# First block's gate and value products in unsplit float32, and a front in a new order

## The chip, the cores and the metric

One core of a Trainium2 chip runs the kernel. The metric is the device time of one execution in microseconds; lower is better.

## The reference

A chunked state-space scan makes an array of 3072 tokens by 256 features, and a gated unit follows. All of it is float32.

```python
def _attn_ref(x, a, B, C):            # x (4,8,768,32), a (4,8,768), B and C (4,8,768,16)
    log_a = np.log(np.clip(a, 1e-06, 1.0))
    for c in range(nc):               # chunks of 32 steps
        cum = np.cumsum(la, axis=-1)
        L = np.exp(cum[:, :, :, None] - cum[:, :, None, :]) * causal
        M = np.einsum('bhin,bhjn->bhij', Cc, Bc) * L
        y_intra = np.einsum('bhij,bhjd->bhid', M, xc)
        y_inter = np.einsum('bhin,bhnd->bhid', Cc, state) * np.exp(cum)[..., None]
        y[:, :, sl] = y_intra + y_inter
        state = decay_full * state + np.sum(Bx, axis=2)   # Bx: B times x, decayed to the chunk's end
def _moe_ref(x, w_gate, w_val, w_out):                    # 256 -> 1536 -> 256
    g = x @ w_gate
    silu = g * (1.0 / (1.0 + np.exp(-g)))
    return (silu * (x @ w_val) @ w_out)
```

## The kernel before

**Blocks.** The 768 steps are cut into NB = 6 blocks of 128 steps; a block holds the 4 batches, so T = 512 tokens. Inside a block the scan works on K = 2 pieces of Q = 64 steps. For each block there are three stages: the attention, the gate and value products with SiLU and their product (NF = 12 units of 128 hidden features), and the output product (12 units, two halves of the output features).

**The attention of a block.** The decays a come as rows. For blocks 0 and 1 they are loaded small (`load_rows`), clipped, spread over the partitions by a float32 matmul against a 0/1 matrix `pick` (`spread`, the records "a") and scanned from PSUM by VectorE in halves (`scan_spread`) into L (decay between two steps) and E (decay from the piece's start). For blocks 2 to 5 the clipped rows are written to DRAM once (`load_all`, `clip_all`, `write_all`) and then loaded broadcast over the partitions (`load_aj`, `load_an`) and scanned there (`scan_j`, `scan_n`). `scores` makes S from B and C, C split by heads into Cz (`heads_apart`); `mix` multiplies S into L; `sums` makes the pieces' own states st from B weighed by the decay (`weigh_b`); `apart` and `step` make the running states T; `values` and `carried` add up y in PSUM, the latter with C weighed by E (`weigh_c`). All matmuls of the attention are float32 on small tiles.

**The split products.** The gated unit works in fp32r, a shorter float. Each operand is split into a high and a low part, and a product is three matmuls: high by high, low by high, high by low. For x that is `x_high` and `x_low`. The weights come as packed 8-byte numbers, in 18 pieces of 512 KB: 12 gate/value pieces (wg0 to wg11) and 6 output pieces (wo0 to wo5). Each goes through `w_magnitude`, `w_range`, `w_rest`, `w_shift`, `w_sign`, `w_round` to a float32 tile "w", then `w_high` and `w_low`; four or five of these must be VectorE's, the others may be ScalarE's. The hidden activations sg are split as well (`hid_high`, `hid_low`) just ahead of the output product.

**Order.** A planner (`Plan`) writes the order of the instructions by a list schedule: each operation has an engine or a choice of two, a cost, a rank (about the time when it is due), what it needs, and which buffers of a pool it takes and gives back. The engines then run their instructions in that fixed order, each waiting on semaphores. `due` and `due_sum` give the ranks of the products: blocks 0 and 1 form a group, and their gate products alternate unit by unit, so that a weight piece is used twice when it is ready; then come both output stages, and after these the blocks one at a time. `idle` puts filler matmuls on a tile of ones ("rest") into TensorE's stream, in groups of 6; `IDLE = 7, 12` groups. All loads go through SyncE's queue. All calls pass through one wrapper, so every row of the trace has its line, 192, and groups are told apart by their tiles: gv are the gate and value sums, po the output sums.

Of the kernel before, what the change touches and what calls it, by code (L numbers as in the profile page):

```python
# [29 lines left out]
SG = 21  # L30
# [172 lines left out]
def scan_moe_kernel(ctx: ExitStack, tc, aj, an, bc, xb, wgv, wo, cst, sel, out):  # L203
# [23 lines left out]
    pick = const.tile([K * BATCH, BATCH + 1, P], F32, name="pick")  # L227
# [4 lines left out]
    bl = [dict() for _ in range(NB)]  # L232
# [8 lines left out]
    def load_rows(k):  # L241

        t = moe.tile([K * BATCH, 2, T + 32], F32, tag="xl", name=f"rows{k}")
        t = bl[k]["rows"] = t[:, :, : H * W]
        sp.dma_start(t[:, 0], aj[k].rearrange("q (b c) -> (q b) c", b=BATCH))
        sp.dma_start(t[:, 1], an[k])
# [47 lines left out]

    def scan(t, d):

        ve.tensor_tensor_scan(t, t, d, 0.0, ALU.mult, ALU.add)

    def clip_rows(k, i):
        clip(bl[k]["rows"][:, i].rearrange("p (g t) -> p g t", t=W)[:, :, 1:])  # L300
# [3 lines left out]
    def spread(k, b, i):  # L304

        t = bl[k]["spread", b, i] = ps_at.tile([P, HALF], F32, tag="at", name=f"a{k}_{b}_{i}")
        src = bl[k]["rows"][:, b // BATCH, HALF * i : HALF * i + HALF]
        te.matmul(t, pick[:, b], src, start=True, stop=True)

    def scan_spread(k, b, i):  # L310
        if b < BATCH:
            to, d = bl[k]["L"][:, H * b : H * b + H], dj
        else:
            to, d = bl[k]["E"].rearrange("p b q t -> p (b q) t"), dn
        to, d = (t.rearrange("p g t -> p (g t)") for t in (to, d))
        half = slice(HALF * i, HALF * i + HALF)
        ve.tensor_tensor_scan(to[:, half], bl[k]["spread", b, i], d[:, half], 0.0, ALU.mult, ALU.add)
# [26 lines left out]
    def weigh_c(k):  # L344
        t = bl[k]["C"].rearrange("p b (q i) -> p (b q) i", i=Q)
        E = bl[k]["E"].rearrange("p b q t -> p (b q) t")
        ve.tensor_tensor(out=t, in0=t, in1=E[:, :, :Q], op=ALU.mult)

# [74 lines left out]
    def values(k, b):  # L423

        c = bl[k]
        if not b:
            c["y"] = [
                t[:, : BATCH * Q].rearrange("p (b i) -> p b i", i=Q) for t in banks(k, "y", 2 * K)
            ]
        L = c["L"].rearrange("p (b h) t -> p b h t", h=H)  # L430
        for g in range(2):
            for h in range(4 * g, 4 * g + 4):
                for q in range(K):
                    o = D * (h % 4)
                    te.matmul(
                        c["y"][2 * q + g][o : o + D, b], c["x"][piece(q), b, D * h : D * h + D],
# [19 lines left out]
    def new_x(k):  # L456
        xh[k] = moe.tile([P, 2, T], F32R, tag="xh", name=f"xh{k}")
        t = moe.tile([P, 2, T + 32], F32R, tag="xl", name=f"xl{k}")
        xl[k] = t.rearrange("p g t -> p (g t)")[:, : 2 * T].rearrange("p (g t) -> p g t", g=2)

# [27 lines left out]
    def w_magnitude(i, e):  # L488
        w = part[i]["w"] = raw.tile([P, 4 * P], I32, tag="w", name=f"{pieces[i][4]}w")
# [101 lines left out]
    def idle(n, i):  # L591
# [3 lines left out]
        for _ in range(6):  # L595
# [3 lines left out]
    load_rows(0)  # L599
    sp.dma_start(pick, sel)  # L600
    sp.dma_start(cs, cst)
    warm = const.tile([P, 1], F32, name="warm")
# [6 lines left out]
    def do(f, *a):  # L609
# [4 lines left out]
        dict(mm=4, at=4, L=1, E=1, bc=1, xb=1, Cz=1, T=2, tmp=2, raw=3, w=3, x=2, hh=HB, sg=SG, ob=2),  # L614
        dict(SP=3.0, Act=3.0, DVE=1.0, PE=1.5, Pool=2.0, **{"-": 0.0}),
# [6 lines left out]
    begin, t = {}, FIRST  # L622
    for g in groups:
        for i, k in enumerate(g):
            begin[k] = (t, i, len(g))
        t += len(g) * NF * ((GV if g[0] else PACE0) + PO) + len(g) * ATT

    def due(k, f=0):

        t, i, n = begin[k]  # L630
        return t + (f * n + i) * (GV if k > 1 else PACE0)

    def due_sum(k, f):
        t, i, n = begin[k]
        return t + n * NF * (GV if k > 1 else PACE0) + (i * NF + f) * PO

    add("-", 0.0, lambda: None, -9, gives="pick", lag=0.2)
    add("Act", 0.6, lambda: se.copy(dj, eye.unsqueeze(1).to_broadcast([P, H, W])), -9, ["cs"], gives="dj")
    add("-", 0.0, lambda: None, -9, gives="cs", lag=0.4)


    for n, many in enumerate(IDLE):
        for i in range(many):
            need = [("idle", n, i - 1)] if i else [("M", 0, 0)] if n else []
            takes = [] if i else [("at", ("rest", n))]
            add("PE", 0.37, do(idle, n, i), i if not n else 15 + i, need, takes=takes, uses=[("rest", n)], gives=("idle", n, i), kind="r")


    for i in range(NW):
        r = due(0, i) - 1.0 if i < NF else due_sum(0, 2 * (i - NF)) - 1.0  # L650
        add("SP", 0.48, do(w_fetch, i), r - 9.0, takes=[("raw", ("raw", i))], gives=("raw", i), lag=1.75)
        add([("Act", 0.6), ("DVE", 0.335)], None, do(w_magnitude, i), r - 5.5, [("raw", i)], takes=[("w", ("w", i))], gives=("mag", i))
# [4 lines left out]
        add("DVE", 0.6, do(w_round, i), r - 3.3, [("sign", i), ("rest", i)], uses=[("raw", i)], gives=("round", i))  # L657
        add([("Act", 0.6), ("DVE", 0.36)], None, do(w_high, i), r - 2.7, [("round", i)], gives=("wh", i))
# [165 lines left out]
```

## Time and profile before

| | us |
|---|---|
| runs, median of 3 (lowest, highest) | 375.75 (374.13, 378.84) |
| profiled execution | 375.97 |
| its span, first to last instruction | 374.2 |
| busy in the span: TensorE, weight loads, VectorE, ScalarE | 364.0, 288.9, 231.3, 129.3 |

The span is what the trace covers; 1.77 us of the profiled execution lie outside it. Busy shares are means over stages that have different limits, and a busy TensorE may still be running at its lower clock level, so equal instructions of different stretches have to be compared by their lengths.

### The profile page before, as it was taken

To read this page: it belongs to the slowest core of one execution; us is meant where nothing else is said; L and a number is where in the kernel's file an instruction comes from. 1 tells how busy PE (TensorE), PEld (TensorE's weight loads), DVE (VectorE), ACT (ScalarE), POOL (GpSimd) and SP (SyncE) were. 2 spreads that over 40 slices of the span, in tenths; PEclk is the share of its full clock that TensorE was granted. 3 is DMA by queue.
4 is the path that set the end of the run, shared out by engine and by line. 5 is a ranking of instruction groups with operands and counts; after the bars stand their busy time and mean duration, and the time that the engine had idled before them with its cause. 6 is when DMAs were issued, how large, how long until landed. Compare 5 with 4: busy or idle time off the path is not lost.

```text
span 374.2 us, 7684 instructions
## 1 busy us (share of the span) xinstructions
PE 364.0 (97%) x3342; PEld 288.9 (77%) x3342; DVE 231.3 (62%) x416; ACT 129.3 (35%) x230; POOL 0.8 (0%) x6
## 2 busy tenths in 40 slices
PE   7999998899999999899999999999999999999996
PEld 5677676687878877687778887788887788888896
DVE  4789996899997545269548564447763445262241
ACT  3244354366633542223134222134212134222142
POOL 0000000000000000000000000000000000000000
PEclk9999999999999999699999999999999999999999
DMA  6233169634400100560055100064100000100001
GB/s 258 90 103 154 60 182 232 175 116 145 134 0 0 58 0 34 156 154 2 4 164 121 57 0 2 4 176 108 56 3 2 2 2 0 56 2 0 0 2 56
DMA packets 8193, 26.81 MB, mean 72 GB/s; under 512 B 952, under 2 KB 1848, under 8 KB 7648
## 3 DMA queue, kind: packets, MB, share of 16 engines
q1 hardware_dynamic: 8160, 26.33, 23.5%
q8 instruction: 26, 0.43, 0.5%
q14 instruction: 7, 0.06, 0.1%
HBM read 22.98 MB, written 3.35 MB: 70 GB/s over the span
## 4 chain that ended last, share of the span: by engine, by line
PE 78%; DVE 14%; DMA 4%; issue 2%; ACT 0%; SPq 0%; DVEq 0%; ACTq 0%
PE gv L192 38%; PE po L192 27%; PE y L192 4%; DMA wg8r<-in_wgv 4%; PE a L192 4%; DVE sg L192 2%; PE rest L192 2%; PE S L192 2%; DVE L L192 2%; PE st L192 1%; DVE wo4w L192 1%; DVE wg5w L192 1%; DVE wo5w L192 1%; DVE wg11w L192 1%; DVE wg8w L192 1%
## 5 line engine op out<-in xcount | busy, mean ns | idle before, releaser
L192 DVE TENSOR_TENSOR sg<-gv,sg 128x512 f32<-128x512 f32 x72 | 49.8, 692 | 77.2 <-PE gv L192 77.1
L192 ACT ACTIVATE sg<-gv 128x512 f32<-128x512 f32 x72 | 42.5, 594 | 94.0 <-PE gv L192 93.9
L192 DVE TENSOR_TENSOR hl<-sg,hh 128x512 fp32r<-128x512 f32 x72 | 49.4, 689 | 29.0 <-ACT hh L192 28.5
L192 ACT CAST hh<-sg 128x512 fp32r<-128x512 f32 x58 | 36.1, 623 | 56.7 <-PE po L192 27.9
L192 DVE TENSOR_TENSOR_SCAN L<-L,dj 128x520 f32<-128x520 f32 x16 | 19.7, 1239 | 5.0 <-DMA L<-clipped 5.0
L192 PE MATMUL a<-rows,pick 8*128 8x260 f32 x40 | 16.1, 539 | 0.9 <-DVE rows L192 0.9
L192 DVE TENSOR_TENSOR L<-S,L 128x512 f32<-128x512 f32 x24 | 15.1, 685 | 2.8 <-PE S L192 2.8
L192 ACT COPY ob<-po 128x512 f32<-128x512 f32 (+1 forms) x13 | 7.2, 555 | 21.3 <-PE po L192 20.8
L192 DVE TENSOR_TENSOR_SCAN L<-a,dj 128x260 f32<-128x260 f32 x16 | 10.9, 694 | 4.3 <-PE a L192 4.2
L192 PE MATMUL y<-L,xb 64*32 64x64 f32 x768 | 11.9, 236 | 1.8 <-issue 1.3
L192 PE MATMUL rest<-unit 128*128 128x128 bf16 x114 | 11.8, 273 | 1.1 <-DVE warm L192 1.1
L192 PEld LDWEIGHTS <-unit 128*128 128x128 bf16 x114 | 9.2, 124 | 4.5 <-issue 3.3
L192 PEld LDWEIGHTS a<-rows,pick 8*128 8x128 f32 x40 | 9.1, 252 | 4.4 <-DVE rows L192 1.2
L192 PEld LDWEIGHTS y<-L,xb 64*32 64x32 f32 x768 | 7.9, 112 | 4.3 <-issue 1.7
L192 PEld LDWEIGHTS y<-bc,T 32*64 32x64 f32 x352 | 7.5, 140 | 4.3 <-issue 2.6
L192 PE MATMUL y<-bc,T 32*64 32x64 f32 x352 | 10.5, 239 | 0.0
L192 PE MATMUL po<-hh,wo0h 128*128 128x512 f32 (+1 forms) x26 | 9.8, 377 | 0.2 <-DVE sg L192 0.2
L192 PE MATMUL po<-hh,wo4h 128*128 128x512 f32 (+1 forms) x26 | 9.9, 382 | 0.0
L192 PE MATMUL po<-hh,wo3h 128*128 128x512 f32 (+1 forms) x26 | 9.9, 382 | 0.0
L192 PE MATMUL po<-hh,wo5h 128*128 128x512 f32 (+1 forms) x26 | 9.8, 378 | 0.0
L192 ACT ACTIVATE Cz<-bc,cs 128x512 f32<-128x512 f32 x10 | 6.7, 716 | 8.8 <-DMA bc<-in_bc 8.8
L192 PE MATMUL po<-hl,wo4h 128*128 128x512 f32 (+1 forms) x26 | 9.7, 374 | 0.0
(258 smaller groups left out, 823.0 us busy)
## 6 DMA issues: line engine op xcount, KB each, us to landing
xb<-in_xb SPq DMA_DIRECT2D x6, 768.0 KB, 7.5
L<-clipped SPq DMA_DIRECT2D x8, 520.0 KB, 7.8
bc<-in_bc SPq DMA_DIRECT2D x6, 512.0 KB, 3.7
out<-ob SPq DMA_DIRECT2D x11, 256.0 KB, 2.0
E<-clipped SPq DMA_DIRECT2D x4, 260.0 KB
wg0r<-in_wgv SPq DMA_DIRECT2D x1, 512.0 KB, 6.1
wg1r<-in_wgv SPq DMA_DIRECT2D x1, 512.0 KB
wg2r<-in_wgv SPq DMA_DIRECT2D x1, 512.0 KB
```

What stands on the lines that cost most here:

```text
L192: ins = getattr(self.engine, name)(*a, **k)
```

## The change

Block 0 runs its gate and value products alone and first. They take x as plain float32 copies of y (`x_whole`) and the rounded weights "w" as they are, in two float32 matmuls in place of six fp32r ones. The high and low parts of the gate weights are made later, before block 1's products, and `w_low` then waits for block 0's product with that piece. Until then the piece's float32 tile sits in the pool of the hidden activations (sg, 22 buffers in place of 21). The order of the large stages becomes: gate 0, gate 1, output 0, output 1, gate 2, output 2, and so on.

In the front, only batches 0 to 2 of block 0's L are spread by matmuls; batch 3 and E are loaded broadcast from the input and clipped and scanned in place. Block 1 uses the loads from DRAM like the later blocks. Block 0's bc and xb are issued from ScalarE's queue. The copy of `dj` goes from ScalarE to VectorE. `values` of block 0 runs in two halves by heads, each after two of the four `mix`. `weigh_c` of block 0 covers only the second piece. The filler groups have 3 matmuls in place of 6, in another number and at other ranks (46 groups in all). Block 2's attention and its loads get earlier ranks, the loads behind the fetch of piece 14.

```diff
-SG = 21
+SG = 22
...
+    def load_first_aj():
+        t, c = bl[0]["L"][:, H * SPREAD :], SPREAD * H * W
+        for q in range(K):
+            sp.dma_start(
+                t[piece(q)].rearrange("p g t -> p (g t)"),
+                aj[0, q, c:].unsqueeze(0).to_broadcast([Q, BATCH * H * W - c]),
+            )
+    def load_first_an():
+        sp.dma_start(
+            bl[0]["E"].rearrange("p b q t -> p (b q t)"),
+            an[0].unsqueeze(1).to_broadcast([H, N, BATCH * K * W]),
+        )
...
-        sp.dma_start(t, bc[k])
+        (sp if k else se).dma_start(t, bc[k])
...
-        sp.dma_start(t, xb[k])
+        (sp if k else se).dma_start(t, xb[k])
...
+    def x_whole(i, e):
+        copy(e, x_part(whole[0], i), bl[0]["y"][i])
...
     def gate_val(k, f, m):
+        if not k:
+            w = part[f]["w"].bitcast(F32).rearrange("p (a b c) -> p a b c", b=2, c=P)
+            for kc in range(2):
+                te.matmul(t, w[:, m, kc], whole[0][:, kc], start=not kc, stop=kc == 1)
+            return
         runs = [(w, x, kc) for w, x in ((wgh, xh), (wgl, xh), (wgh, xl)) for kc in range(2)]
...
-        for _ in range(6):
+        for _ in range(3):
             te.matmul(rest[n], unit, unit, start=True, stop=True)
...
-    GV, PO, ATT = 2.82, 1.41, 5.0
-    FIRST, PACE0 = 16.0, 3.2
-    groups = [(0, 1), *((k,) for k in range(2, NB))]
+    GV, PO, ATT, FIRST, PACE0 = 2.82, 1.41, 5.0, 17.0, 3.75
+    for k in range(NB):
+        begin[k] = t
+        t += (NF * GV if k else NF * PACE0) + ATT
+        for i in (() if not k else (0, 1) if k == 1 else (k,)):
+            begin_sum[i] = t
+            t += NF * PO
...
+        if i < NF:
+            r = due(1, i) - LATER
         add([("Act", 0.6), ("DVE", 0.36)], None, do(w_high, i), r - 2.7, [("round", i)], gives=("wh", i))
-        add("DVE", 0.6, do(w_low, i), r - 1.5, [("wh", i)], uses=[("w", i)], gives=("wl", i))
+        whole_done = [("gv", 0, i, m) for m in range(2)] if i < NF else []
+        add("DVE", 0.6, do(w_low, i), r - 1.5, [("wh", i), *whole_done], uses=[("w", i)], gives=("wl", i))
...
-        if k < 2:
-            z = (-5, 17)[k]
+        z = -5 if not k else r + LEAD[min(k, 3)]
...
-            z = r - 44 + 22 * (k == 2)
...
+        late = [("raw", LATE[k])] if k in LATE else []
...
-IDLE = 7, 12
+SPREAD = 3
+IDLE = [-9.0] * 8 + [-3.1, -3.0, -2.9, -2.8] + [0.5 * i for i in range(10)], [15.0 + 0.5 * i for i in range(24)]
+ALL, LATER = 16.0, 3.0
+LEAD = {1: -30.0, 2: -44.0, 3: -44.0}
+LATE = {2: NF + 2}
```

## Rows read from the trace of the kernel before

**Rows 1.** Stretches: window, length, busy us of PE, PEld, DVE, ACT, POOL, then clock, DMA.

```profile
0.00:28.10 28.10, 26.12 (x387) 19.14 (x388) 18.84 (x40) 10.33 (x20) 0.84 (x6) 1.00 0.42 151
28.10:111.40 83.30, 80.07 (x664) 62.20 (x664) 78.12 (x155) 40.68 (x74) 0.00 (x0) 1.00 0.46 134
111.40:153.30 41.90, 39.94 (x466) 30.64 (x465) 22.91 (x38) 15.77 (x28) 0.00 (x0) 0.99 0.07 27
195.19:250.30 55.11, 55.11 (x538) 44.17 (x537) 31.47 (x53) 15.85 (x28) 0.00 (x0) 1.00 0.21 57
```

**Rows 2.** Chain that ended last, the front: start us, us, engine and tile.

```profile
7.99 2.03 PE a L192 x4
...
12.80 1.94 PE S L192 x64
14.74 0.61 PE st L192 x32
...
20.32 1.98 PE y L192 x121
22.30 2.04 PE rest L192 x18
24.33 1.06 PE y L192 x32
...
26.15 1.51 PE a L192 x6
...
28.10 2.82 PE gv L192 x12
...
32.42 0.78 PE rest L192 x12
```

**Rows 3.** The same chain, from 150 us on.

```profile
150.78 1.27 issue
...
153.30 19.42 PE gv L192 x72
...
195.19 16.32 PE po L192 x72
211.51 16.32 PE gv L192 x72
```

**Rows 4.** The loads and VectorE's steps in the gate stage: timeline, chain, groups.

```profile
54.62 1.20 SPq L192 DMA_DIRECT2D L<-clipped  x2
...
56.85 14.88 DMA wg8r<-in_wgv
...
76.46 0.60 DVE wg8w L192
77.06 0.34 DVE wg9w L192
...
L192 DVE TENSOR_TENSOR sg<-gv,sg 128x512 f32<-128x512 f32 x72 | 49.8, 692 | 77.2 <-PE gv L192 77.1
```

**Rows 5.** Timeline of TensorE, a gap in the gate stage, in brackets.

```profile
65.28 0.73 PE L192 MATMUL gv<-xh,wg4h 128*128 128x512 f32 x2 [1.14 <-ACT sg L192]
```

**Rows 6.** Timeline of the front, loads and their first users.

```profile
2.28 0.43 SPq L192 DMA_DIRECT2D bc<-in_bc  x1
...
4.75 1.49 DVE L192 TENSOR_TENSOR_SCAN L<-a,dj 128x260 f32<-128x260 f32 x2 [1.32 <-PE a L192]
...
6.18 1.33 ACT L192 ACTIVATE Cz<-bc,cs 128x512 f32<-128x512 f32 x2 [1.89 <-DMA bc<-in_bc]
...
9.35 0.66 ACT L192 ACTIVATE wg0w<-wg0r 128x512 f32<-128x512 f32 x1 [1.83 <-DMA wg0r<-in_wgv]
```

**Rows 7.** A stretch of the front, columns as in the first group; last is GB/s.

```profile
3.00:6.00 3.00, 2.56 (x6) 2.08 (x7) 1.56 (x3) 0.63 (x1) 0.00 (x0) 1.00 0.90 325
```

**Rows 8.** Instructions of two tiles, ns min/median/max: "a" from 26 us, then gv.

```profile
L192 PEld LDWEIGHTS a<-rows,pick x20: 181/184/185, 26.1 to 40.0; 8*128 8x128 f32 x20
...
L192 PEld LDWEIGHTS gv<-xh,wg0h x16: 187/188/333, 153.3 to 322.9; 128*128 128x128 f32 x16
```

More of the change, by code (lines that the diff above doesn't have):

```diff
@@ L231, in scan_moe_kernel @@
     clipped = dram.tile([2, P, NA * W], F32, name="clipped")
-    bl = [dict() for _ in range(NB)]
+    bl = [dict(y={}) for _ in range(NB)]
     def copy(e, to, src):
@@ L344, in weigh_c @@
     def weigh_c(k):
[L345 to L347 removed]
+        t = bl[k]["C"].rearrange("p b (q i) -> p b q i", i=Q)
+        E = bl[k]["E"][:, :, :, :Q]
+        if k:
+            t, E = (v.rearrange("p b q i -> p (b q) i") for v in (t, E))
+        else:
+            t, E = t[:, :, 1], E[:, :, 1]
+        ve.tensor_tensor(out=t, in0=t, in1=E, op=ALU.mult)
     def banks(k, name, n):
@@ L488, in w_magnitude @@
     def w_magnitude(i, e):
-        w = part[i]["w"] = raw.tile([P, 4 * P], I32, tag="w", name=f"{pieces[i][4]}w")
+        w = part[i]["w"] = (
+            moe.tile([P, T], I32, tag="sg", name=f"{pieces[i][4]}w", bufs=SG) if i < NF
+            else raw.tile([P, T], I32, tag="w", name=f"{pieces[i][4]}w", bufs=2)
+        )
         if e == "Act":
@@ new lines, in scan_moe_kernel, with behind, load @@
+        z = -5 if not k else r + LEAD[min(k, 3)]
+        L, E, BC, XB, CZ, TT = ("L", k), ("E", k), ("bc", k), ("xb", k), ("Cz", k), ("T", k)
+        add("-", 0.0, do(new_decays, k) if k else lambda: None, z - 12, [("decays", k - 1)] if k else [], takes=[("L", L), ("E", E)], gives=("decays", k))
+        late = [("raw", LATE[k])] if k in LATE else []
+        def behind(key):
+            return [(key, k - 1)] if k else []
+        q = ("SP", 0.48) if k else ("-", 0.0)
+        def load(f):
+            return do(f, k) if k else lambda: None
@@ L714, in scan_moe_kernel @@
         for p in range(NP):
-            add("DVE", 0.6, do(mix, k, p), z + (8 if k else 4.5) + 0.5 * p, [*done, *(("L", k, b) for b in range(BATCH)), *(("bt", k, b) for b in range(BATCH))], uses=[S[p]], gives=("M", k, p))
+            add("DVE", 0.6, do(mix, k, p), z + 8 + 0.5 * p if k else (-1.25, -1.24, -1.1, -1.1)[p], [*done, *(("L", k, b) for b in range(BATCH))], uses=[S[p]], gives=("M", k, p))
         before = [("step", k - 1, K - 1)] if k else []
@@ L739, in scan_moe_kernel @@
             need = [*xs, ("wh", f), ("wl", f)]
+            c = 1.4
+            if not k:
+                need = [("round", f), *(("xf", i) for i in range(2 * K))]
+                c = 1.85
             gv = [("gv", k, f, m) for m in range(2)]
             for m in range(2):
-                add("PE", 1.4, do(gate_val, k, f, m), r + m * 0.1, need, takes=[("mm", gv[m])], uses=[("x", k), gv[m]], gives=gv[m], kind="r")
+                add("PE", c, do(gate_val, k, f, m), r + m * 0.1, need, takes=[("mm", gv[m])], uses=[gv[m], ("x", k) if k else "xf"], gives=gv[m], kind="r")
             t = ("sg", k, f)
@@ L804 @@
     cst[:, W + 2 :] = odd[:, None] == (np.arange(2 * D) // D)[None, :]
-    sel = np.zeros((K * BATCH, BATCH + 1, P), np.float32)
+    sel = np.zeros((K * BATCH, SPREAD, P), np.float32)
     row = np.arange(K * BATCH)[:, None]
-    for b in range(BATCH):
+    for b in range(SPREAD):
         sel[:, b] = row == BATCH * (p // Q) + b
-    sel[:, BATCH] = row == p // N
     ins = dict(aj=aj, an=an, bc=bc, xb=xb, wgv=wgv, wo=wo, cst=cst, sel=sel)
```

170 lines of the change are left out of this document (91 added, 79 removed).

## The prediction

> **What bounds the kernel now.** I read the time in four stretches and asked of each which engine has no room [rows 1]: 0 to 28.1 us, the front, until the first gated-unit product starts; 28.1 to 111.4, the gate and value products of blocks 0 and 1 taken in turns; 111.4 to 153.3, their output products and block 2's attention; and then a period of 55.11 us per block. In the last one TensorE is busy all the time, so nothing but fewer or shorter matmuls could help there, and the change touches none of them. The time to win is ahead of 153.3.
>
> The chain of waits through the front [rows 2] is nearly all TensorE. Look at the length of equal things: 18 filler matmuls ("rest") take 2.04 us at 22.30, 0.113 us each, but 12 take 0.78 at 32.42, 0.065 each; the spreading matmul of 8 rows ("a") takes 0.507 us per record at 7.99 and 0.252 at 26.15. So TensorE runs at its lower level (1.2 GHz) until about 26.1 and at 2.4 GHz after, although the page's clock row shows full speed there; I trust the durations. What it did just before the rise was rest and y, from 22.30 to 26.15. Between 28.1 and 111.4 the chain goes over VectorE, which is busy for 78.1 of 83.3 us [rows 1]: it splits 18 weight pieces and feeds two blocks. A piece also came late: 14.88 us from issue to landing, issued 2.2 us behind the decay loads of block 2 [rows 4], and gaps such as the 1.14 us at 65.28 [rows 5] follow (there is a second, similar one nine us later).
>
> The useful work after 28.1 can be counted. 72 matmuls of 512 columns take 16.32 us in either kind of product [rows 3], so 0.2267 each; a block needs 144 for gate and value (32.64) and 72 for the output (16.32). The period of 55.11 less 48.96 is 6.15 for one block's attention on TensorE, handovers included. From 28.1 to 153.3 pass 125.2 us; the work in it is 65.28 + 32.64 + 2 x 6.15 = 110.2. So 15.0 are lost there. Right behind, block 2's first 72 matmuls take 19.42 in place of 16.32: 3.1 more, since the engine stood for 1.27 at 150.78 and came back at the lower level [rows 3]. From 153.3 to the end would be 220.9 - 3.1 = 217.8.
>
> **The change part by part.** *Block 0 in float32.* It removes six products per unit and puts two float32 ones in their place: 48 in all. The trace has no dense float32 product of 128 x 512. The nearest for the kind is "a": 20 calls leave 40 records, and a record of 260 columns takes 0.252 us at the full level [rows 2], against 0.115 for 260 columns at the fp32r rate. So a call is two records of two passes each; one pass for all is excluded by this row. Four passes at the rate of the same shape are 4 x 0.2267 = 0.907; scaling "a" by columns gives 2 x 0.252 x 512 / 260 = 0.992. I take 0.907, the same shape: 48 x 0.907 = 43.5, that is 10.9 more than the 32.64 of before; the other end is 47.6.
>
> *Splitting put off.* The first gate product no longer waits for the high and low parts, but for the rounded piece and four plain copies of x. For a gate piece VectorE now owes four operations ahead of its product, 0.34 + 0.34 + 0.60 + 0.60 by the steps between starts [rows 4], 1.9 us per unit, against 2 x 1.81 = 3.6 of TensorE. For the gate stage of block 0 with block 1's attention beside it, TensorE needs 43.5 + 6.15 = 49.7. VectorE needs 10.5 pieces x 1.9 = 20, 12 products x 0.6 = 7.2, two low parts 1.2, and block 1's attention: the period's 31.5 busy [rows 1] less 24 products and low parts of 0.69 [rows 4] is 14.9. That is 43 of 49.7: it fits. In block 1's gate stage (32.6) it owes 10 low parts, 12 products, six output pieces of 2.5 and four hidden low parts, 30.6; what doesn't fit can follow in the output stage, where 20 hidden low parts and block 2's attention make 27 of 38.8. So VectorE stops being the bound, but in the middle stage only just. The deferred low part waits for block 0's product, and products of VectorE are queued behind it; it is due some three units later, so I charge nothing, and a product's 0.6 where it is late. The pieces now hold sg buffers, 22 for 12 pieces and 24 hidden tiles: at block 0's last two units a buffer comes free only through a low part; 1 to 2 us if VectorE is behind.
>
> *Spreads and loads.* Block 0 keeps 6 of 10 spreading calls, block 1 none of 10 (20 records, 0.252 each at the full level [rows 2], 5 us of TensorE, gone). For it come two broadcasts and two full scans for block 0 and, for block 1, the decay loads that blocks 2 and later have. That is 0.53 MB more in the front; at 325 GB/s [rows 7] 1.6 us for whatever is queued behind, which is the first weight piece. That piece was ready at 9.35, far ahead of its use, and it still is. The copy of dj moves to VectorE, which stood 1.32 us before its first scan at 4.75 [rows 6]: hidden, 0.6 if not. The two large loads move to ScalarE's queue: 0.43 us of issue each, and ScalarE waits for one of them anyway. bc was issued at 2.28 and its first user started at 6.18 [rows 6]; issued at about 1, it would serve at 5. I count nothing for this, because TensorE isn't waiting for it. In the Trainium skill, DMA: Bandwidth & Descriptors, Issuing engines are not separate DMA queues, says that transfers started by different engines share the same 16 DMA engines and that only issue time is saved; by that the 1.3 MB come no sooner than the rate lets them, and my sum, which has no term for them, stays. No run here shows it yet.
>
> *The front.* By the ranks, TensorE's program ahead of the first product is 46 groups of 3 rest matmuls, 12 "a" records, S, two lots of st and the two lots of y. At the lower level [rows 2]: 138 x 0.113 = 15.6, 12 x 0.507 = 6.1, 1.9, 1.2, 2.0 + 1.1, together 27.9; from 1.05 on it ends at 28.9, no sooner than now. All hangs on when the level rises. 24 rests come first (to 3.8), then four calls of "a" (8), S (10.3), three groups and the last "a" (13.4), then ten groups in a row, st and y. Only there does the program look as it did from 22.30 to the rise at 26.15; I place the rise where as much of that is done, at 17.3, and call it a guess with wide ends. By then 16.25 of the 27.9 are done, and the other 11.65 shrink by 0.065 / 0.113 to 6.7: first product at 24.0, 4.1 sooner. Bounds: 28.9 if it never rises; if the first 24 rests already raise it, at about 4.9, TensorE's work alone ends at 4.9 + 24.05 x 0.575 = 18.7, and with handovers to VectorE such as the 1.32 before the first scan [rows 6] I take 20.5.
>
> *Block 2's attention* is placed earlier and all in the output stage; the 1.27 gap and the lower level behind it (3.1) go.
>
> **Sum.** 24.0 + 49.7 (gate 0, attention 1) + 32.6 (gate 1) + 38.8 (output 0 and 1, attention 2) + 217.8 = 362.9. For losses in place of the 15.0 I put 2.4, one gap like that at 65.28 and one like that at 150.78. The span is 365.3, and with the 1.77 that lie outside it in the profiled execution (375.97 against 374.2) 367.1. That execution stands 0.2 above the median of the runs, 375.75, so no correction: 2.3% less.
>
> **The rivals.** (1) *The front gains nothing:* the level rises as late as now, and the new fillers are paid at 0.113. First product at 28.5, 371.6. For it: in the trace shorter filler lots didn't raise it; against: the longer lot behind the last "a". (2) *The loss moves into block 0's stage:* block 1's bc, xb and decay loads, 2.6 MB, are released together when block 0's attention ends, and a piece behind them lands as late as the one of 14.88; with the shared buffers some 5 us more than my 2.4, 372.1. Against: three pieces are fetched ahead, and a unit now takes 3.6. (3) *The level rises early:* 20.5, 363.6. (4) *Slower:* the weight loads of the float32 products don't hide. 96 records, each with 0.187 [rows 8] ahead of it, are 18.0 us: 385.1. It decides for slower from 0.17 per record. Against: in "a" a load of 0.181 and a matmul of 0.252 repeat every 0.252 at the full level, so it is hidden there. The Trainium skill, TensorE: Matmul & The Clock Gate, Weight-path perf modes, says that the fast weight load is not used for float32 operands; by that the loads could be longer than the split kind's. The rows show 0.181 for 8 x 128 float32 and 0.187 for the split kind [rows 8], no difference; if it held, rival 4 is its result. That the change doesn't do what it says (VectorE stays the bound) is inside rival 2.
>
> **How the numbers follow.** About 2% is what a measurement of this kernel can tell from no change: 368.2 and 383.3. Forecast 0.52, with 362 to 372 as its own range (front 21.5 to 27, losses 0.5 to 5, float32 up to 0.95); 0.38 of it lies below 368.2. Rival 3 has 0.12, rival 1 0.17, rival 2 0.13, rival 4 0.06. Faster 0.38 + 0.12 = 0.50, same 0.14 + 0.17 + 0.13 = 0.44, slower 0.06. The range is 360 to 376: it takes in the first three rivals and the dearer float32, and leaves out rival 4 and the far ends.
>
> **What would show it.** In the new profile: gate products of block 0 as pairs of records of about 0.45 us with no gap for weight loads; rest at 0.065 from about 17 us; the first product at 24; VectorE below 90% in block 0's stage; no product of block 1 waiting for a piece's low part; and block 2's gate at full level. I am wrong if float32 takes more than 0.95 per product, if the level falls again in block 0's stage, or if the pieces' loads end last there.

## The result

The changed kernel takes 371.12 us in the median (369.22 to 374.25), the kernel before 375.49 on the same chip (373.67 to 380.48): a ratio of 0.989, 95% interval 0.9855 to 0.9925. That is 1.1% less, where 2.3% and 367.1 us were forecast. The direction was right, the size was not. It is also less than the 2% that the prediction named as what such a measurement can tell from no change (faster had 0.50 there, same 0.44), though the interval lies clear of 1. 371.12 lies inside the range of 360 to 376, but that range holds the unchanged time of 375.49 too, so this says little. The profiled execution took 371.95 with a span of 370.2, against 365.3 in the sum.

The stretches of the changed kernel, in the columns of [rows 1]: the front, gate 0 with block 1's attention, gate 1, both outputs with block 2's attention, and the rest.

```profile
0.00:25.84 25.84, 21.27 (x402) 16.77 (x403) 15.99 (x34) 8.71 (x17) 0.84 (x6) 1.00 0.47 147
25.84:79.26 53.42, 50.16 (x456) 24.07 (x453) 50.56 (x99) 28.96 (x52) 0.00 (x0) 1.00 0.63 189
79.26:112.42 33.16, 33.16 (x146) 27.00 (x144) 31.31 (x56) 13.97 (x24) 0.00 (x0) 1.00 0.31 99
112.42:151.51 39.09, 38.81 (x466) 31.11 (x466) 28.33 (x49) 14.86 (x26) 0.00 (x0) 1.00 0.30 82
151.51:370.20 218.69, 215.30 (x1828) 174.28 (x1827) 104.82 (x174) 60.37 (x106) 0.00 (x0) 1.00 0.14 37
```

Set beside the sum's 24.0, 49.7, 32.6, 38.8 and 217.8 (with 2.4 of losses): the last three are met within 1 us each, the first two are longer. Against the kernel before, the front is 2.26 shorter (28.10 is the chain's figure; in the timeline the first product stood at 27.91, so like for like it is 2.07); from the first gate product to block 2's gate pass 125.67 us, as before (125.2), though block 0's products take 8.7 us longer in it; and the rest is 2.21 shorter. Block 2's first 72 products are at the full level this time, and the 1.27 gap ahead of them [rows 3] is gone. This is one execution of 16: the mean granted clock is 1.000 in seven of them and 0.977 to 0.995 in the other nine (0.991 in the profile of before), so what the others do there isn't shown.

```profile
147.88 3.63 PE po L192 x16
151.51 16.32 PE gv L192 x72
```

The chain through the front, as in [rows 2]. It no longer begins on TensorE but with a load:

```profile
1.53 5.79 DMA cs<-in_cst
7.32 0.02 issue
7.34 0.44 DVE dj L192
...
7.89 0.71 DVE L L192
...
10.30 1.94 PE S L192 x64
12.24 1.07 PE rest L192 x9
13.32 2.03 PE a L192 x4
15.34 3.31 PE rest L192 x30
...
19.05 0.66 PE rest L192 x9
...
22.27 1.60 issue
```

The same beginning in the timeline, as in [rows 6]; what ended an idle time is in brackets:

```profile
0.73 0.39 ACTq L192 DMA_DIRECT2D bc<-in_bc  x1
1.14 0.50 ACTq L192 DMA_DIRECT2D xb<-in_xb  x1
...
4.88 2.93 PE L192 MATMUL a<-rows,pick 8*128 8x260 f32 x6 [1.09 <-DMA pick<-in_sel]
...
7.34 0.43 DVE L192 COPY dj<-cs 128x520 f32<-128x520 f32 x1 [3.66 <-DMA cs<-in_cst]
7.41 1.33 ACT L192 ACTIVATE Cz<-bc,cs 128x512 f32<-128x512 f32 x2 [4.24 <-DMA cs<-in_cst]
7.89 1.29 DVE L192 TENSOR_TENSOR_SCAN L<-a,dj 128x260 f32<-128x260 f32 x2
```

Read three things. The constants cs take 5.79 us from issue to landing, so the first scan starts at 7.89 and not at 4.75 [rows 6], and Cz at 7.41, not 6.18, though bc was issued 1.55 us sooner. In the 3 us of [rows 7] the DMA engines are now full:

```profile
3.00:6.00 3.00, 1.91 (x11) 1.47 (x9) 0.41 (x1) 0.17 (x1) 0.00 (x0) 1.00 1.00 375
```

And 30 fillers at 15.34 take 0.110 each, nine at 19.05 take 0.073: the level rises near 18.6, where I had put 17.3.

In block 0's stage the products look as forecast, in steps of 3.44 per unit with a weight load (in the last line, as in [rows 8]) that costs nothing, until loads come late (compare [rows 5]):

```profile
48.68 3.60 PE L192 MATMUL gv<-xf,wg6w 128*128 128x512 f32 x8
52.20 0.46 PE L192 MATMUL st<-xb 64*32 64x64 f32 x32
54.72 0.35 PE L192 MATMUL st<-xb 64*32 64x64 f32 x16 [2.06 <-DVE xb L192]
...
59.75 1.96 PE L192 MATMUL gv<-xf,wg8w 128*128 128x512 f32 x4 [0.78 <-DVE wg8w L192]
```

```profile
L192 PEld LDWEIGHTS gv<-xf,wg0w x8: 190/190/192, 25.8 to 28.5; 128*128 128x128 f32 x8
```

The gap of 2.06 ends with VectorE's weighing of xb, which stands behind a scan of L and the steps of wg7. VectorE itself had stood for loads, once for L and once (through ScalarE's first step) for wg7:

```profile
46.93 2.37 DVE L192 TENSOR_TENSOR_SCAN L<-L,dj 128x520 f32<-128x520 f32 x2 [1.08 <-DMA L<-clipped]
...
50.36 0.43 DVE L192 TENSOR_SCALAR wg7w<-wg7w 128x512 f32<-128x512 f32 x1 [0.48 <-ACT wg7w L192]
```

Ahead of that, SyncE's queue, as in [rows 4]. Block 1's bc and xb go out at 24.64 and 26.28, its decays, 1.3 MB, between wg6 and wg7, and wg7 needs 10.89 us (the chain's line, last).

```profile
35.38 1.14 SPq L192 DMA_DIRECT2D L<-clipped  x2
36.56 0.63 SPq L192 DMA_DIRECT2D E<-clipped  x1
38.75 0.33 SPq L192 DMA_DIRECT2D wg7r<-in_wgv  x1
```

```profile
38.75 10.89 DMA wg7r<-in_wgv
```

### The profile page after: what moved, and what is told of

It reads as the page before. It is cut to its first block, busy times and chain, and to the rows that moved or that the text cites. A ratio compares the mean times of both kernels' runs of the same rounds, so it can differ in the third digit from the quotient of the medians.

```text
span 370.2 us, 7586 instructions
## 1 busy us (share of the span) xinstructions
PE 358.7 (97%) x3290; PEld 273.2 (74%) x3290; DVE 231.0 (62%) x410; ACT 126.9 (34%) x224; POOL 0.8 (0%) x6
## 4 chain that ended last, share of the span: by engine, by line
PE 75%; DMA 13%; DVE 8%; issue 2%; SPq 1%; ACT 0%; DVEq 0%; ACTq 0%
PE gv L192 46%; PE po L192 19%; PE y L192 5%; DMA xb<-in_xb 3%; DMA wg7r<-in_wgv 3%; DMA L<-clipped 3%; DVE L L192 2%; DMA wg4r<-in_wgv 2%; PE S L192 2%; DMA cs<-in_cst 2%; PE rest L192 2%; PE st L192 1%; DVE hl L192 1%; PE a L192 1%; SPq L192 1%
## 5 line engine op out<-in xcount | busy, mean ns | idle before, releaser
L192 ACT CAST hh<-sg 128x512 fp32r<-128x512 f32 x55 | 34.2, 622 | 45.5 <-PE po L192 35.2
L192 DVE TENSOR_TENSOR_SCAN L<-L,dj 128x520 f32<-128x520 f32 x21 | 25.7, 1230 | 5.2 <-DMA L<-clipped 5.2
L192 PEld LDWEIGHTS <-unit 128*128 128x128 bf16 x138 | 11.0, 121 | 4.7 <-issue 3.5
L192 PE MATMUL rest<-unit 128*128 128x128 bf16 x138 | 12.8, 264 | 1.0 <-DVE warm L192 1.0
L192 PE MATMUL po<-hl,wo2h 128*128 128x512 f32 (+1 forms) x26 | 9.9, 380 | 0.3 <-DVE hl L192 0.3
L192 PE MATMUL po<-hl,wo3h 128*128 128x512 f32 (+1 forms) x26 | 9.9, 381 | 0.1
L192 PE MATMUL po<-hh,wo2h 128*128 128x512 f32 (+1 forms) x26 | 9.8, 378 | 0.0
L192 PE MATMUL po<-hh,wo2l 128*128 128x512 f32 (+1 forms) x26 | 9.7, 374 | 0.0
L192 PE MATMUL po<-hh,wo3l 128*128 128x512 f32 (+1 forms) x26 | 9.7, 374 | 0.0
L192 PE MATMUL po<-hh,wo0l 128*128 128x512 f32 (+1 forms) x26 | 9.7, 374 | 0.0
```

The costliest lines, as they stand in the source:

```text
L192: ins = getattr(self.engine, name)(*a, **k)
```

## The experiments

Two questions: what made the front late, and what sets the end of block 0's stage. For the front the theory was that the small loads land late because large ones run beside them; its rival, that TensorE's own program at the lower level sets it. For the stage the theory was that pieces come late; its rivals, that TensorE's longer float32 products or VectorE's steps set it. All ratios are to the kernel before on the same chip and come from all runs; times within a run are those of its one profiled execution. "First product" is the first gate product, gate 1 the first product of block 1, block 0's stage the time between the two, and "outputs" the first output product.

**One queue.** bc and xb go back to SyncE's queue, at the same place in the program.

```diff
-        (sp if k else se).dma_start(t, bc[k])
+        sp.dma_start(t, bc[k])
...
```

> The changed kernel with bc and xb of block 0 issued from SyncE's queue again, at the same place, behind cs and the broadcasts. Theory A (the front's gain was eaten by small loads that land late beside the large ones: cs landed at 7.32 us, pick held the first spread until 4.88): cs lands before 4.5, the first spread starts before 4.0, the first scan before 6.0, and the first gate product starts 1.5 to 3 us sooner than the 25.84 of the changed kernel; time about 369. Rival B (fillers and the clock level alone set the front): the loads land sooner, but the first gate product stays within 0.7 us of 25.84; time unchanged, 371.

Ratio 0.9876 (0.9821 to 0.9931), not to be told from the changed kernel's 0.989. cs came early again (dj's copy at 3.44, first scan 4.99), but now bc, queued behind the broadcasts, was the late one: Cz at 9.52, S at 10.91, first product at 26.42. So the two large loads on ScalarE's queue were what held cs up. But one wait took the other's place, and what the front loses by it this run alone doesn't show.

**Small loads first.** As above, and bc ahead of the broadcasts of L and E: the order is then rows (16.2 KB), pick (12), cs (65.5), bc (512), the broadcasts and xb. bc isn't small, but the chain waits for it.

```diff
+    load_bc(0)
     load_first_aj()
     load_first_an()
-    load_bc(0)
...
```

> The changed kernel with all front loads on SyncE's queue in the order rows, pick, cs, bc, broadcasts, xb. The run with bc and xb behind the broadcasts had cs early (3.4) but bc late (9.5), and TensorE stood 2.9 us for it. Theory A: with both early, the first spread starts at 3.7, S starts before 9, the first gate product starts 1.5 to 2.5 us before 25.84; the time falls by less, 0 to 2 us (369 to 371), if block 0's stage is limited by its loads (theory C), and by all of it if not.

Ratio 0.9861 (0.9806 to 0.9916), span 366.6. TensorE's timeline of the front:

```profile
3.72 3.83 PE L192 MATMUL a<-rows,pick 8*128 8x260 f32 x8
...
7.92 2.01 PE L192 MATMUL S<-Cz,bc 32*64 32x128 f32 x64
...
12.96 3.33 PE L192 MATMUL rest<-unit 128*128 128x128 bf16 x30
...
20.85 0.69 PE L192 MATMUL y<-bc,T 32*64 32x64 f32 x31 [1.18 <-issue]
...
22.82 1.51 PE L192 MATMUL gv<-xf,wg0w 128*128 128x512 f32 x3
```

By the timelines S starts 2.3 us sooner than in the changed kernel, the same 30 fillers come 2.3 sooner, the first product 3.0 sooner, and the span is 3.6 shorter. One profile of each is little to go by, but more runs below have either front with the same fillers: the nine with this order have the first product at 21.36 to 24.02 (mean 23.2), the three with the changed kernel's at 25.29 to 25.84 (mean 25.6). So the order of the loads cost the front some 2.4 us. In the time of whole runs it is less clear: 0.9861 for 0.989 is 1.1 us, and the intervals overlap.

**Fillers early.** The same with 36 more fillers at the start.

```diff
-IDLE = [-9.0] * 8 + [-3.1, -3.0, -2.9, -2.8] + [0.5 * i for i in range(10)], [15.0 + 0.5 * i for i in range(24)]
+IDLE = [-9.0] * 20 + [-3.1, -3.0, -2.9, -2.8] + [0.5 * i for i in range(10)], [15.0 + 0.5 * i for i in range(24)]
```

> The kernel with the small loads first, and 36 more rest matmuls right at the start (60 in place of 24 ahead of the first spreading call). If a long dense stretch of rest is what raises the level, as the 30 in a row at 13 us did, rest falls from 0.113 to 0.07 each at 5 to 7 us, the spreading calls take 0.25 per record in place of 0.5, S 1.0 in place of 2.0, and the first gate product starts at 20 to 21 in place of 22.8. The rival, that the waits on VectorE's scans bring the lower level back, or that it never rises there: the 36 cost 36 x 0.07 to 0.113 = 2.5 to 4.1 us, and the first gate product starts at 24 to 27.

Ratio 0.9842 (0.9788 to 0.9895), first product at 23.91: close to the rival's time, though the level did rise. 60 fillers took 4.78, the spreading records 0.25 each from 5.76 on, S 1.21. But then TensorE waited for VectorE (1.20 at 14.17), stood 1.76 at 19.85 with nothing shown that it waited for, and its last 24 fillers were back at 0.113. The run isn't clean: with the longer lot the planner put VectorE's scan of the broadcast batch ahead of the spread ones, and VectorE stood 3.27 for that load, so its first scan began only at 7.49. In this order, and with 36 fillers more to pay, the higher level in the front was worth little.

**No late fillers.** The second lot (24 groups of 3, due between the first units) is gone.

```diff
-IDLE = [-9.0] * 8 + [-3.1, -3.0, -2.9, -2.8] + [0.5 * i for i in range(10)], [15.0 + 0.5 * i for i in range(24)]
+IDLE = [-9.0] * 8 + [-3.1, -3.0, -2.9, -2.8] + [0.5 * i for i in range(10)], []
```

> The changed kernel without the second lot of 24 filler groups (72 rest matmuls; 36 of them ran ahead of the first gate product and 36 between block 0's units). If they are only paid for, the 2.5 us between block 0's units go, and up to 2 us ahead of the first product: 367 to 369. If they hold up the clock level, the level rises later or falls again and block 0's first products take 0.86 us per record in place of 0.43: first product later than 26, time 371 to 375.

Ratio 0.9933 (0.9893 to 0.9973). First product 1.54 sooner, at 24.30, but block 0's stage is 54.12: a gap of 3.29 at 48.70 ahead of wg6, and then 5.37 in place of 3.60 for its products. The fillers stood where TensorE would have waited anyway.

**Block 0 split again**, alone and first as in the change, with the six fp32r products and the low parts ahead of them.

```diff
-        if not k:
-            w = part[f]["w"].bitcast(F32).rearrange("p (a b c) -> p a b c", b=2, c=P)
-            for kc in range(2):
-                te.matmul(t, w[:, m, kc], whole[0][:, kc], start=not kc, stop=kc == 1)
-            return
...
-        if i < NF:
-            r = due(1, i) - LATER
...
-        add("DVE", 0.6, do(w_low, i), r - 1.5, [("wh", i), *whole_done], uses=[("w", i)], gives=("wl", i))
+        add("DVE", 0.6, do(w_low, i), r - 1.5, [("wh", i)], uses=[("w", i)], gives=("wl", i))
...
```

> The changed kernel with block 0's gate and value products in split form again (three products with high and low parts of x and of the weights made ahead), block 0 still alone and first. TensorE then needs 32.6 us for the stage where it now needs 41.3, VectorE 12 low parts more ahead of the products. Theory A (VectorE is the limit when the splitting lies ahead): the stage from the first product of block 0 to the first of block 1 takes 50 to 54 us all the same and the front is 1 to 3 us longer: 372 to 376. Rival B (VectorE has room, float32 is a net cost): the stage falls to 45 us or less: 363 to 367.

Ratio 1.0003 (0.9959 to 1.0046). From the first product to gate 1 TensorE is busy for 44.83 of 54.83 us, in place of 50.16 of 53.42, VectorE for 52.61: the saved TensorE time is not seen, it becomes waits for high and low parts (2.51 at 51.67 for wg6h is the longest). So the whole 1.1% hangs on float32 with the low parts put off; the two were changed together, and which of them counts isn't shown.

**The decays written early**, in the front, in the changed kernel and in the one with the small loads first.

```diff
-    add("DVE", 0.3, clip_all, ALL + 4, ["all"], gives="clipped")
-    add("SP", 0.48, write_all, ALL + 5, ["clipped"], gives="written", lag=1.5)
+    add("DVE", 0.3, clip_all, -1.6, ["all"], gives="clipped")
+    add("SP", 0.48, write_all, -1.0, ["clipped"], gives="written", lag=1.5)
```

> The changed kernel with the clip and the write of all decays moved from after the first gate product (25.88 and 27.29 us) into the front, where the DMA queue is empty. Theory C (block 0's stage is limited by what its loads let through: the write landed some 8 us after issue behind 2.3 MB, so block 1's decays were issued at 35.4, landed at 46.9, and piece wg7 behind them at 49.6): decays issued before 29, wg7 landed before 47, the stage from the first product of block 0 to that of block 1 falls from 53.4 to 50 to 52, time 368.5 to 370. Rival D (the fixed order or TensorE's own work sets the stage): stage within 0.7 us of 53.4, time 371.

> Both: front loads in the order rows, pick, cs, bc, broadcasts, xb, and the early clip and write of the decays. Theories A and C together: first gate product at 23.5 to 24.5, stage 50 to 52, 366.5 to 368.5. If block 0's stage isn't limited by its loads, no better than the better one of the two alone.

Ratios 0.9962 (0.9929 to 0.9995) and 0.9891 (0.9849 to 0.9932), stages 55.04 and 55.05. The decay loads now go out ahead of wg4 and the following pieces, and the same gap comes earlier: 2.08 at 44.52, or 41.63, for wg4, and after it 5.24 or 5.37 for eight products. Moving the burst only moves the wait.

**Four raw buffers** in place of three (and 20 sg buffers, for room).

```diff
-    raw = pool("raw", 3)
+    raw = pool("raw", 4)
...
```

> The changed kernel with four buffers for raw weight pieces in place of three, paid for with two of the 22 sg buffers. Theory C (pieces late in block 0's stage): four pieces instead of three are on the chip when the burst of block 1's loads begins, no gap of over 1 us behind wg7; stage 50.5 to 52.5; time 369 to 370.5. Rival E (the buffers shared by pieces and hidden tiles limit the end of the stage): units 10 and 11 wait for buffers, gaps of 1 to 3 us there, time 371 to 374.

Ratio 0.9867 (0.9824 to 0.991). The stage is 52.21, 1.2 shorter; wg7 goes out at 31.87, ahead of block 1's decays, and the gap of 2.06 is gone, but one of 1.79 (for T, ScalarE's) stands at 60.66. The ratio alone is not to be told from 0.989.

**Both**: small loads first and four raw buffers; then the same with half of the second filler lot (the cut shown).

```diff
-IDLE = [-9.0] * 8 + [-3.1, -3.0, -2.9, -2.8] + [0.5 * i for i in range(10)], [15.0 + 0.5 * i for i in range(24)]
+IDLE = [-9.0] * 8 + [-3.1, -3.0, -2.9, -2.8] + [0.5 * i for i in range(10)], [15.0 + 0.5 * i for i in range(12)]
```

> The small loads first in the front, and four raw buffers with 20 sg buffers. If the two losses are separate (a late front, and pieces that come late in block 0's stage), the gains of the two runs alone add up: first gate product at 22.8 and a stage of 52.2 in place of 53.4, so gate 1 starts at about 75.0, the span is 370.2 - 3.0 - 1.2 = 366.0, and the ratio to the kernel before about 0.982. The rival, that the stage's end is set by when the pieces land, counted from the start and not from the first product: gate 1 starts no sooner than at 76 to 77, the stage grows to 53.5 or more, and the ratio stays at 0.986.

> The same with 36 rest matmuls fewer in the second lot. If these fillers only cover waits (as the run without the whole lot suggested), gate 1 starts within 0.5 us of the run with the whole lot and the ratio is the same within 0.3%. The rival, that they take TensorE's time in the first units, 36 x 0.07 = 2.5 us: gate 1 starts 2 us sooner, and the ratio is 0.5% lower.

Ratios 0.9797 (0.9755 to 0.9839) and 0.9805 (0.9749 to 0.986): the two best versions that leave nothing out, medians 368.23 and 368.93. First product at 23.15, gate 1 at 75.36 and a span of 366.5 for the first, nearly as expected; but its outputs start at 109.98, no sooner than with the small loads alone (109.90), so how much of the better ratio is the buffers' stays unsure. With fewer fillers gate 1 starts at 72.84, 2.5 sooner, as that rival had it, but its stage grows from 34.62 to 36.72 (a gap of 1.36 at 84.67 for VectorE's sg), and the outputs start at 109.56 against 109.98. What is won ahead of gate 1 is lost in it.

**Less load.** Small loads first, and three of four batches of block 1's L not loaded; VectorE's steps stay as long.

```diff
-                t[piece(q)].rearrange("p g t -> p (g t)"),
-                src[k, q].unsqueeze(0).to_broadcast([Q, BATCH * H * W]),
+                t[piece(q), : H if k == 1 else BATCH * H].rearrange("p g t -> p (g t)"),
+                src[k, q, : H * W if k == 1 else BATCH * H * W].unsqueeze(0).to_broadcast([Q, (1 if k == 1 else BATCH) * H * W]),
...
```

> The kernel with the small loads first, but three of the four batches of block 1's L are not loaded (0.8 of the 1.06 MB); VectorE scans batch 0's decays in their place, with equally long steps. Left out: the decays of batches 1 to 3 of block 1. If the weight pieces come late in block 0's stage because block 1's loads lie ahead of them, 0.8 MB at 243 GB/s are 3.3 us: wg7 and wg8 land 2 to 3 us sooner, the gap of 1.75 goes, and gate 1 starts 1.5 to 2.5 us sooner, at about 74. The rival, that VectorE's steps set the stage (it is busy for 50.6 of 53.4 us): gate 1 starts within 0.5 us of 75.9 though the pieces land sooner.

Ratio 0.9815 (0.9769 to 0.986). The loads did come sooner, as the view of the DMA issues from 20 to 62 us shows (KB each, then the median us from issue to landing), first without and then with the cut:

```profile
L<-clipped SPq DMA_DIRECT2D x2, 520.0 KB, 9.2
...
wg7r<-in_wgv SPq DMA_DIRECT2D x1, 512.0 KB, 10.7
```

```profile
wg7r<-in_wgv SPq DMA_DIRECT2D x1, 512.0 KB, 5.6
...
L<-clipped SPq DMA_DIRECT2D x2, 130.0 KB, 4.3
```

Gate 1 starts at 75.59, only 0.34 sooner; the rival that VectorE sets it has this time right. But this run's first product came at 24.02, 1.2 later, with its first unit at the lower level (4.55 for 3.65), so the stage has to be taken by itself. From the first product to gate 1, in the columns of [rows 1], first without and then with the cut:

```profile
22.82:75.93 53.11, 50.16 (x456) 24.07 (x453) 50.84 (x100) 29.02 (x52) 0.00 (x0) 1.00 0.59 187
24.02:75.59 51.57, 50.96 (x454) 24.49 (x453) 49.47 (x96) 27.57 (x50) 0.00 (x0) 0.98 0.56 173
```

TensorE stands for 0.61 us of the stage in place of 2.95. The longest gap without the cut, 1.75, is gone, and the one for wg8, 0.78, is 0.18:

```profile
51.38 0.35 PE L192 MATMUL st<-xb 64*32 64x64 f32 x16 [1.75 <-DVE xb L192]
```

```profile
56.08 1.96 PE L192 MATMUL gv<-xf,wg8w 128*128 128x512 f32 x4 [0.18 <-DVE wg8w L192]
```

VectorE never stood for 0.2 us or more between 28.67 and 108.95, and yet TensorE hardly waited for it. So the waits in this stage hung on the loads, and the rival's time came out by the late start and the slow first unit; with that unit at 3.65 the stage would be 50.7 (an estimate, 51.57 less 0.90).

**No gate low parts** on VectorE, 12 steps less; the products take the high parts in their place.

```diff
-        lo = wts.tile([P, 4 * P], F32R, name=f"{name}l")
+        lo = hi if i < NF else wts.tile([P, 4 * P], F32R, name=f"{name}l")
+        if i >= NF:
...
```

> The kernel with the small loads first, without the 12 low parts of the gate weights on VectorE (12 x 0.6 = 7.2 us, most of them in block 0's stage); their matmuls use the high parts. Left out: the low parts of the gate weights. The order of all other instructions is kept. If VectorE sets the end of the two gate stages, the output products start 3 to 4.5 us sooner, at 105.4 to 107 in place of 109.9: 105.4 is where TensorE's own work ends (22.8 + 41.3 + 6.15 + 2.5 + 32.6). The rival, that the loads set it: within 1 us of 109.9.

Ratio 0.9784 (0.971 to 0.9857), outputs at 110.71: the rival, that the loads set it. (The profiled execution, 369.43, is the slowest of this version's four; their median is 368.01.) VectorE, relieved, stands and waits for pieces, as the list of waits from 20 to 112 us shows (engine, for what, total us):

```profile
ACT wg7w L192 <- DMA wg7r<-in_wgv: 4.1, 1, 4.1
...
ACT wg6w L192 <- DMA wg6r<-in_wgv: 3.4, 1, 3.4
DVE wg6w L192 <- ACT wg6w L192: 2.8, 1, 2.8
```

TensorE stands for 3.92 of the stage's 55.41 us, more than with the low parts (2.95 of 53.11), though it also began 1.5 us sooner.

**Neither**: no gate low parts and less load.

> Both at once on the kernel with the small loads first: three of four batches of block 1's L not loaded, and no low parts of the gate weights (their matmuls use the high parts). Left out: these decays and these low parts. If loads and VectorE each hide the other, TensorE alone is left in block 0's stage: 41.3 of float32 products, 2.5 of fillers and 6 to 7 of attention, 50 to 51 after the first product; with that at 21.5 to 23 gate 1 starts at 72 to 73.5 in place of 75.9, the output products at 105 to 106.5, and no gap over 0.6 us stands in the stage. The rival, that something else sets the stage: gate 1 at 75 to 77 as in each run alone.

Ratio 0.9767 (0.9708 to 0.9826), span 364.9. From the first product to gate 1, and gate 1's stage:

```profile
23.90:74.12 50.22, 49.92 (x455) 24.20 (x453) 47.10 (x94) 29.08 (x52) 0.00 (x0) 1.00 0.59 186
74.12:108.08 33.96, 33.96 (x211) 27.74 (x209) 29.56 (x51) 14.52 (x24) 0.00 (x0) 1.00 0.33 96
```

The stage is 50.22 with TensorE busy for 49.92 of it, so it stands for 0.30; less load alone left 0.61 of standing, no low parts alone 3.92, neither cut 2.95. Gate 1 starts at 74.12 where less load alone had 75.59, but 0.9 of these 1.47 us are the first unit, here at the full level. So the loads alone make nearly all of the waits in block 0's stage, and the low parts on VectorE add 0.3 us at most. The rest is TensorE's own work, about 50 us. The ratios of the four versions (0.9861, 0.9815, 0.9784, 0.9767) have intervals that overlap and don't rank them.

**Low parts on GpSimd**, with the small loads first, and with the four raw buffers and fewer fillers.

```diff
-        ve.tensor_tensor(
+        (ge if i < NF else ve).tensor_tensor(
...
```

> The kernel with the small loads first, with the 12 low parts of the gate weights on GpSimd, which has no work after the front. If VectorE sets the stages and GpSimd's steps slow nothing, the output products start at 106 to 108 in place of 109.9 and the span is 363 to 365 in place of 366.6. The rival, that GpSimd's steps hold up VectorE's (no row here shows the two at work at once on large tiles) or take several us each: 110 or later, span 366.6 or more.

> The same move to GpSimd in the kernel with the small loads first, four raw buffers and half of the second lot of fillers (span 366.0, output products at 109.6). If VectorE sets the stages there too, the 36 fillers that are gone now count: output products at 104 to 106.5, span 361 to 363.5, ratio about 0.97. The rival as in the run before: 109 or later, and no gain.

Ratios 1.0038 (0.9997 to 1.0078) and 0.9997 (0.9959 to 1.0034): all of the gain lost. VectorE's steps of 30 to 60 us in the first of them, mean ns before the bar:

```profile
L192 DVE TENSOR_TENSOR sg<-gv,sg 128x512 f32<-128x512 f32 x6 | 4.0, 674 | 0.0
...
L192 DVE SCALAR_TENSOR_TENSOR wg6w<-wg6r,wg6w 128x512 int32<-128x512 int32 x1 | 1.8, 1752 | 0.0
L192 DVE SCALAR_TENSOR_TENSOR wg4w<-wg4r,wg4w 128x512 int32<-128x512 int32 x1 | 1.6, 1645 | 0.0
```

The same step on wg6w takes 687 ns in the kernel with VectorE's low parts.

**Block 2 at its old, late ranks**, in the changed kernel and in the version with fewer fillers.

```diff
-LEAD = {1: -30.0, 2: -44.0, 3: -44.0}
-LATE = {2: NF + 2}
+LEAD = {1: -30.0, 2: -22.0, 3: -44.0}
+LATE = {}
```

> The changed kernel with block 2's attention and its loads at the ranks they had before (22 us ahead of its products, not 44, and its loads not held behind a weight piece). Prediction's step (the gap and the lower clock level around 150 us went because this attention was moved): a gap of over 1 us returns ahead of block 2's gate product and its first 72 matmuls take 19 us in place of 16.3: 374 to 376. Rival (they went for another reason, or came from one execution's accident): within 0.5% of the changed kernel, 369.5 to 373.

> The kernel with the small loads first, four raw buffers and half of the second lot of fillers, with block 2's loads and attention at their old, late ranks, so that VectorE does block 2's scans behind block 1's gate products. If VectorE holds up block 1's gate stage there (36.7 us for 32.6 of products), that stage shrinks to 33 to 34.5, output products start at 106 to 107.5, and the output stage grows by at most 1.5: span 364 to 365.5, ratio about 0.972. The rival, that what VectorE no longer does early is missing later: the output stage grows by 2 to 3 and the span stays at 366.

Ratios 0.992 (0.9884 to 0.9955) and 0.9832 (0.9781 to 0.9884), both within 0.5% of their pairs (0.989 and 0.9805). The gap ahead of gate 2 did not come back. In the first, block 0's stage is 51.20 in place of 53.42, but gate 1 and the outputs take 73.91 in place of 72.09 (by the timelines), so the earlier ranks bought nothing that these runs show. In the second, gate 1's stage shrinks from 36.72 to 34.46 as expected, but the output stage grows from 38.24 to 39.79, and the span is 366.9: most of it is given back.

## Why the forecast was too low

The span is 4.9 us over the sum. By its own terms:

- **The float32 products were mis-sized, in the kernel's favour.** Steps of 0.43 us per record, 0.86 per product, 41.3 for 48 in place of 43.5: 2.2 less. Rival 4 is out: a weight load of 0.190 lies beside a record of 0.43. The Trainium skill, TensorE: Matmul & The Clock Gate, Weight-path perf modes, says that the fast weight load is not used for float32 operands; these rows show no difference by it (0.187 for the split kind [rows 8]).
- **The front is the step that failed**: "The two large loads move to ScalarE's queue ... I count nothing for this". I asked what sits behind them on their own queue and who waits for bc, and not what loads issued at the same time then share. cs and pick landed late, the scans started 3.1 us later, and everything behind them. The first product came at 25.84, and 36 of the 138 fillers that I had put ahead of it ran between units 0 and 3 (1.34 + 0.33 + 0.83 = 2.5): 4.3 over the sum's 24.0 in all. The run with the small loads first gives back 3.0 of it in its profile, and the means of the two fronts are 2.4 apart. Of the 1.3 to 1.9 that are left the cause is open; TensorE's stand of 1.60 at 22.27, for which the profile shows no reason, is of that size. The prediction had cited the Trainium skill, DMA: Bandwidth & Descriptors, Issuing engines are not separate DMA queues, that transfers started by different engines share the same 16 DMA engines, and used it only to say that bc comes no sooner. The trace agrees with it (the DMA share is 1.00 at 3 to 6 us), and more follows from it than I took: the small loads pay. Fewer fillers are no cure for this: without the second lot the first product came 1.54 sooner, but the stage behind it grew, and the ratio is 0.9933.
- **The guess at the level** was a lesser matter: 18.6 for 17.3. The run with early fillers did not come to what rival 3 gave an early rise (363.6 against its 370.04), but its order had changed and the level fell again; what a rise that lasts would be worth isn't shown.
- **The losses in block 0's stage** are 53.42 - 41.3 - 6.15 - 2.5 = 3.5, where 2.4 was put for all stages. This is rival 2 in kind, and one of the prediction's own signs of being wrong, that the pieces' loads end last: block 1's decays went out just ahead of wg7, which landed after 10.89 us, and with less load TensorE's standing in the stage fell from 2.95 to 0.61. In size it is 1 us, not 5. The count of VectorE, 43 of 49.7, failed as well: it was busy for 50.56 of 53.42, 95% and not below 90%, since the order drew 11 low parts, not 2, and some of the hidden ones into this stage. "VectorE stops being the bound" held even so for this stage: with all of VectorE's steps in place and less to load, TensorE stood for only 0.61 us.
- **Gate 1 and the outputs** (33.16 and 39.09 for 32.6 and 38.8) and the rest (218.69 for 217.8) came as summed. That the gap ahead of gate 2 and its lower level went is right, the reason given is not: with block 2 back at its late ranks they stayed away too. Why they are gone is open; 2.2 of the 4.0 us between the two profiled spans are this, so that more than half of the gain in the profile was forecast for a reason that the runs do not bear out, which is luck.

Added up: 4.3 - 2.2 + 1.1 (stage losses) + 0.6 + 0.3 + 0.9 = 5.0, the 4.9 within rounding.

Where did the 15.0 us of losses go that stood between the first product and gate 2? They were not all waits, as the prediction's word may suggest: TensorE stood for 5.2 of those 125.2 us ([rows 1], 83.30 - 80.07 and 41.90 - 39.94), 14 spreading records of block 1 took 4.1 and 42 fillers 3.2. Of the 15.0 are left 125.67 - 110.2 - 8.7 - 2.5 = 4.3, and TensorE stands for 3.6. But float32's longer products (8.7) and the fillers of the new lot (2.5) took their place, so the stretch is as long as it was. The change makes the work on VectorE ahead of the outputs no shorter either (98.46 us busy up to 113.21, 96.96 up to 111.40 before). What it took out is mostly the spreading, and 1.6 us of waits.

## What to carry to other kernels

When loads move to another queue, list all that is in flight with them, and put what a chain waits for ahead of what nobody waits for yet, whatever queue that has: here 12 and 65.5 KB landed late beside 1.3 MB. When losses on an engine are traded for longer work on it, count first which of them are waits and which are work that the change removes in any case, and count the other engines' work up to the next common point. And judge a stage by its own length and by who stands in it, not by when it ends: where the same front ends up to 2.7 us apart in different executions, a late start can hide that a wait is gone.

## What the hardware showed beside this

- While GpSimd ran the low parts (1.3 to 2.9 us each), five steps of VectorE with both inputs in SBUF that met them between 30 and 60 us took 1.17 to 1.75 us, about 0.69 without. A sixth (hl at 30.08) took 0.68 all the same, and one with a single input, on wg8w at 56.08, took 1.42 for its usual 0.41. The product of gv and sg, one input of which lies in PSUM, stayed at 0.674. The Trainium skill, GPSIMD Engine Reference, Specifications, says that the two share their interfaces to SBUF and contend where VectorE runs in a two-port mode or has two inputs there. The five rows agree; why the sixth was spared, and what mode the step on wg8w ran in, no row shows. An idle GpSimd was worth less than nothing here.
- TensorE stands for 1.2 to 1.9 us at the same instruction of the front, the second part of y from bc and T, in nearly every kernel with this code (1.60 at 22.27 above; 0.58 with the early write), with nothing in the profile that it waits for. What it is stays open.
- The same front, with the small loads first, ended at 21.36 to 24.02 in nine profiled executions. They differ in when the level rose (the first eight spreading records took 2.38 us in the soonest, 2.60 in the next and 3.83 in the other seven) and in the stand just named; a single profile of such a front is good to about 1.3 us either way.
- After a gap of 2.79 to 3.29 us, or of 2.08 in two runs, eight float32 products took 5.0 to 5.4 us; after the 2.06 of the changed kernel and the 2.31 of the run with one queue they took 3.70. Whether a wait of 2 us also costs the level can't be told from its length alone in these rows.
